# Attention and SwiGLU in one kernel: denominators of the first two batches by adds on VectorE, and a new order of gates and values in the front

## The chip, the cores and the metric

The kernel runs on one core of a Trainium2 chip. A core has a matrix engine (TensorE, PE in the profile; PEld is its loading of the stationary operand), three engines that work along rows (VectorE = DVE, ScalarE = ACT, GpSimd = POOL), a queue engine that issues transfers (SyncE = SP) and 16 DMA engines. Each engine takes its instructions in the order in which the program gives them. PE writes its results into eight PSUM banks; DVE and ACT take them out from there ("eviction"). The metric is the device time of one execution in microseconds; the time before the change is 232.76 us, the median of three runs (232.63 to 233.4).

## The reference

Eight batches, 8 heads, 576 positions, 64 features per head, 32 memory slots. Per batch and head:

```python
a   = exp(phi); a = a / sum over positions(a)         # phi: 576 x 32
k_m = a^T k;  v_m = a^T v                             # 32 x 64 each
s   = q k_m^T / 8;  attn = exp(s) / sum over the 32 slots
y   = attn v_m                                        # 576 x 64
```

(The reference also subtracts maxima, which cancel.) The heads' outputs of a position, side by side, are a row x of 512 numbers, 4608 rows in all, and then

```python
out = (silu(x w_gate) * (x w_val)) w_out              # w_gate, w_val: 512 x 1536, w_out: 1536 x 512
```

## The kernel before, in words

**Tiling.** The product of attention and gate or value weights is taken in another order: per batch, U = v_m W (256 rows of head and slot, by 1536 columns, for gate and value each; `u_round`, lines 460 to 502), and then gate^T = U^T attn^T. The 1536 columns come in three chunks of 512; chunk 0 of the weights is loaded in halves of 256 columns (four pieces: gate and value of the first half, then of the second), so that the first U can start earlier. Two row groups g of U (even and odd heads) sit in two banks and are evicted by two instructions; a string such as "va" says which engine takes which ("v" DVE, "a" ACT, with the scale 1/denominator of v_m in the same instruction for batches 0 and 1). `u_half` makes one half of chunk 0, `u_item` a whole chunk for gate and value.

A *slot* s of a batch (24 of them) is 128 of the 1536 columns by 288 positions. `gv_gate` (line 524) multiplies its gate (two matmuls, one for each g) and lets ACT take the silu into a tile `t_sg`, of which there are eight; it then puts a closure into a list `pend`, which, when called, multiplies the value (two matmuls) and lets DVE form silu x value into `t_h`. `flush_mul(n)` calls the oldest n of the list. `gv_slot` makes a gate and then calls what was pending before it, so that gates and values alternate on PE, one slot apart.

**Order of the work.** The program is a hand-written sequence (`manual_schedule`): the order of the Python calls is the order on each engine. Banks are handed out from a list first in, first out (`bank`, `done`, lines 75 to 84), so a bank comes round again after eight uses; `warm` gives its bank back to the front of the list. `warm(n)` (line 862) issues matmuls of the constant block matrix `bones` whose result nobody reads, four of n 128-wide units in each.

**Loads.** phi of batches 0 and 1 goes over the SP and ACT queues. All else is issued by POOL, in this order: k0, q0, k1, q1, v0, v1, the four pieces of chunk 0 (gate, value, gate, value), chunks 1 and 2 of the weights, w_out in three parts with k, phi and v of batch 2 in between. From the ninth of these loads on, POOL waits ahead of an issue until the load eight places earlier has landed.

**Front (batches 0 and 1).** `phi_exp_masked` (line 181) lets ACT write the exponentials of phi into a tile with a zero half: for each j of 9 and each g of 2, 128 columns (4 head pairs x 32 slots), of which only the 64 rows of head g are filled. `kv_denominators` (line 239) sums them for these two batches by 18 matmuls with a vector of ones, and `k_items` takes reciprocals; `direct` multiplies k or v with the exponentials by 36 matmuls into transposed form, which DVE copies to `t_kT`. `q_T` transposes q on PE (three groups of six) and copies it out. `scores` makes q k_m^T and ACT the exponentials E. The inverse sums over the 32 slots come in two ways: `z_inv` (line 418) sums by a matmul with `bones` and lets ACT take ln, ln and exp(-x); `z_inv_v` (line 431) does it on DVE by a summing transpose, a reciprocal and a transpose. `norm` (line 450) multiplies E by the inverse sum into `t_A`. Then come U and the slots of both batches, g0 for batch 0 and g1 for batch 1 (lines 946 to 965), and the third stage: the output product by sums and differences of blocks of `t_h` and `w_out` (`sums`, `weight_sums`, `products`, a seven-product scheme), beside which batches 2 to 7 run.

`phi_sum` (line 205) is there already for later batches: it adds the nine blocks of exponentials on POOL in FP32 and splits the sum into a bf16 high part and a bf16 rest (`t_ehl`), so that the denominators need two matmuls.

The lines around the change are 885 to 966 of the kernel. What decides the order there is this list:

```python
    run([u_half(0, (0,), 0, 0, "va")])
    norm(1, 1)
    run([u_half(0, (1,), 0, 0, "va"), u_half(1, (0, 1), 0, 0, "av")])
    for s in range(4):
        gv_gate(0, s)
    flush_mul(2)
    for s in range(2):
        gv_gate(1, s)
        flush_mul(1)
    run([u_half(0, (0, 1), 0, 1, "va"), u_half(1, (0, 1), 0, 1, "aa")])
    flush_mul(2)
```

Of the kernel before, what the change touches and what calls it, by code (L numbers as in the profile page):

```python
# [9 lines left out]
FP32 = mybir.dt.float32  # L10
BF16 = mybir.dt.bfloat16
# [3 lines left out]
def kernel(  # L15
# [147 lines left out]
    bones = consts.tile([128, 128], BF16, tag="bones", name="bones")  # L163
    ones1 = consts.tile([128, 1], BF16, tag="ones1", name="ones1")
    ones2 = consts.tile([128, NG], BF16, tag="ones2", name="ones2")
# [39 lines left out]
    def phi_sum(b):  # L205
# [14 lines left out]
        esums[b] = hl  # L220

    def kv_sum(b, p, parts):

# [15 lines left out]
    def kv_denominators(b, p):  # L239

        if b in masked:
            for g in range(NG):
                for j in range(JK):
                    nc.tensor.matmul(
                        p[:, g:g + 1],
                        lhsT=masked[b][:, j, g].rearrange("p i m -> p (i m)"),
                        rhs=ones1,
                        start=(j == 0),
                        stop=(j == JK - 1),
                    )  # L250
            return
        if b in esums:
            hl = esums.pop(b)
            terms = [hl[:, t] for t in range(2)]
        else:
            terms = [ephis[b][:, j].rearrange("p i m -> p (i m)") for j in range(JK)]
        for n, x in enumerate(terms):
            nc.tensor.matmul(p, lhsT=x, rhs=ones2, start=(n == 0), stop=(n == len(terms) - 1))
# [190 lines left out]

    def norm(b, g):  # L450
        a = att.tile([128, 2, HALF], BF16, tag=f"A{g}", name="t_A")
        nc.vector.tensor_tensor(out=a, in0=es.pop((b, g)), in1=lzs.pop((b, g)), op=ALU.mult)  # L452
        atts[b, g] = a
# [407 lines left out]

    def warm(n, narrow=0):

# [5 lines left out]
        for a in sizes:  # L869
            nc.tensor.matmul(  # L870
                p[:, 0:128 * a],
                lhsT=bones,
                rhs=x.to_broadcast([128, a, 128]) if a > 1 else bones,
                start=True,
                stop=True,
            )
# [9 lines left out]
    nc.vector.memset(bones, 0.0)  # L886
    nc.vector.memset(ones1, 1.0)
    nc.vector.memset(ones2, 0.0)
# [14 lines left out]
    for c in range(1, NCH):  # L903
        for which in range(2):
            load_w(which, c)
    load_wo(0)
    load_k(2)
    load_wo(1)
    load_phi(2, nc.gpsimd)
    load_wo(2)  # L910
    load_v(2)
    for c in range(NCH):
        u_buffer(1, c, f"S{c}")


    warm(104)
    k0, k1 = k_items(0, "vvvv"), k_items(1, "vvvv")
    q0, q1 = q_items(0, "vav"), q_items(1, "vav")
    run(k0)
    warm(8)  # L920
    run(k1[:1])
    run(q0)
    warm(4)
    scores(0, 0)
# [4 lines left out]
    z_inv(0, 1)  # L929
    norm(0, 0)  # L930
    warm(12)
    run(q1)
    norm(0, 1)
    warm(8)
# [4 lines left out]
    warm(8)  # L939
    z_inv(1, 1)  # L940
    norm(1, 0)
    warm(16)
# [5 lines left out]
    nc.scalar.preload_act_table_set("silu_and_others")  # L948
    run([u_half(0, (0,), 0, 0, "va")])
    norm(1, 1)  # L950
    run([u_half(0, (1,), 0, 0, "va"), u_half(1, (0, 1), 0, 0, "av")])
    for s in range(4):
        gv_gate(0, s)
    flush_mul(2)
    for s in range(2):
        gv_gate(1, s)
        flush_mul(1)
    run([u_half(0, (0, 1), 0, 1, "va"), u_half(1, (0, 1), 0, 1, "aa")])
    flush_mul(2)
    run(g1[2:4] + g0[4:8] + g1[4:6])  # L960
    for c in range(1, NCH):
        s = 8 * c
        run([u_item(0, c)] + g1[s - (2 if c == 1 else 3):s] + g0[s:s + 5])
        run([u_item(1, c)] + g0[s + 5:s + 8] + g1[s:s + 5])
    run(g1[-3:])
# [147 lines left out]
```

## Time and profile before

| what | us |
|---|---|
| median of three runs | 232.76 (232.63 to 233.4) |
| the profiled execution | 232.59, of which the span is 230.8 |
| PE busy | 222.3 (96%) |
| DVE busy | 184.8 (80%) |
| ACT busy | 171.6 (74%) |
| POOL busy | 145.1 (63%) |
| first product with w_out on PE | 54.07 |

The span runs from the first to the last instruction; 1.8 us of the measured time lie outside it. PEclk is the clock that TensorE was granted, in tenths. A row of the timeline gives start, length, engine, line, operation, what is written from what is read, shape and count; in brackets stands how long the engine had been idle before it and what ended that. The rows of groups give busy time in us and the mean of one instruction in ns. Instructions of one row may overlap, so that the length of a row with xN is that of the whole run of N.

### The profile page before, as it was taken

Reading aid. Unit: us, or ns where it says so; the run is one execution under the profiler, and the core shown is the slowest. Engines: PE = TensorE matmul, PEld = TensorE weight load, DVE = VectorE, ACT = ScalarE, POOL = GpSimd, SP = SyncE. Lnnn points to the kernel's source line nnn. Section 1 sums busy time; section 2 is a strip of 40 time slices with the busy share of each in tenths; the row PEclk is TensorE's granted clock in tenths of the full one; section 3 lists DMA queues with packets and bytes.
Section 4 is the critical chain, followed back from the end, with each engine's and each line's share of the span. In section 5 each row is a group of like instructions: output and inputs, shape, how many; then the busy total and the mean of one; then the engine's idle time right before and its main releaser. Section 6 shows DMA issues by size and latency. Waiting matters only on the chain.

```text
span 230.8 us, 7191 instructions
## 1 busy us (share of the span) xinstructions
PE 222.3 (96%) x2818; PEld 169.7 (74%) x2818; DVE 184.8 (80%) x423; ACT 171.6 (74%) x365; POOL 145.1 (63%) x197
## 2 busy tenths in 40 slices
PE   6997799999999999999999999999999999999993
PEld 2554476778887777878788787887788778878882
DVE  4056789999976799989997668998999899977832
ACT  2858898988547989968896658978898789677310
POOL 8422427998099759765977689464845394029291
PEclk9999999999999999999999999999999999999999
DMA  6999999999996993999299964996022602202024
GB/s 213 209 211 206 199 207 207 216 250 266 207 210 176 258 257 69 224 204 177 78 214 195 230 137 110 253 231 101 18 76 102 116 0 95 87 7 91 23 93 162
DMA packets 36546, 36.84 MB, mean 160 GB/s; under 512 B 14496, under 2 KB 30880, under 8 KB 36512
## 3 DMA queue, kind: packets, MB, share of 16 engines
q0 software_dynamic: 16272, 22.42, 52.7%
q1 hardware_dynamic: 19712, 13.37, 22.8%
q10 hardware_dynamic: 528, 0.59, 0.8%
q8 instruction: 22, 0.36, 0.6%
q14 instruction: 12, 0.10, 0.1%
HBM read 42.47 MB, written 9.44 MB: 225 GB/s over the span
## 4 chain that ended last, share of the span: by engine, by line
PE 87%; DMA 9%; POOL 2%; issue 0%; DVE 0%; POOLq 0%
PE p_os L723 21%; PE p_g L515 21%; PE p_v L515 20%; PE p_oc L723 10%; DMA W<-in_moe_w_val_dram 9%; PE p_oa L723 5%; PE p_u L472 5%; PE p_kv L230 2%; PE p_g L396 1%; POOL t_kv L99 1%; POOL t_kv L103 1%; PE p_q L383 1%; POOL t_q L108 0%; POOL W L138 0%; DVE t_q L339 0%
## 5 line engine op out<-in xcount | busy, mean ns | idle before, releaser
L538 DVE TENSOR_TENSOR t_h<-t_sg,p_v 128x288 bf16<-128x288 bf16 x192 | 81.7, 451 | 14.3 <-PE p_v L515 7.3
L515 PEld LDWEIGHTS <-t_U 128*128 128x128 bf16 x768 | 73.9, 98 | 21.2 <-issue 3.5
L532 ACT ACTIVATE t_sg<-p_g 128x288 bf16<-128x288 f32 x192 | 73.2, 424 | 17.2 <-PE p_g L515 11.4
L515 PE MATMUL p_g<-t_A,t_U 128*128 128x288 bf16 x384 | 77.0, 286 | 0.0
L515 PE MATMUL p_v<-t_A,t_U 128*128 128x288 bf16 x384 | 76.9, 286 | 0.0
L723 PEld LDWEIGHTS <-t_S 128*128 128x128 bf16 x384 | 37.3, 98 | 4.5 <-issue 0.2
L603 POOL TENSOR_TENSOR t_S<-t_h 128x512 bf16<-128x512 bf16 x17 | 19.6, 1154 | 27.7 <-DVE t_h L538 26.4
L723 PEld LDWEIGHTS <-t_h 128*128 128x128 bf16 x288 | 27.1, 98 | 8.6 <-issue 5.0
L492 ACT CAST t_U<-p_u 128x512 bf16<-128x512 f32 x51 | 27.0, 606 | 6.4 <-PE p_u L472 6.4
L723 PE MATMUL p_os<-t_T,t_S 128*128 128x256 bf16 x192 | 23.7, 273 | 0.0
L560 POOL TENSOR_TENSOR t_S<-t_S,t_h 128x512 bf16<-128x512 bf16 x17 | 19.6, 1155 | 1.3
L560 POOL TENSOR_TENSOR t_S<-t_h 128x512 bf16<-128x512 bf16 x16 | 18.4, 1152 | 0.0
L560 POOL TENSOR_TENSOR t_S<-t_h,t_S 128x512 bf16<-128x512 bf16 x16 | 18.4, 1151 | 0.0
L472 PE MATMUL p_u<-W,t_kT 64*32 64x512 bf16 (+1 forms) x416 | 15.3, 363 | 1.2 <-DMA W<-in_moe_w_val_dram 0.6
L870 PE MATMUL p_warm<-bones 128*128 128x512 bf16 x44 | 13.6, 450 | 1.7 <-DVE bones L892 1.7
L496 DVE CAST t_U<-p_u 128x512 bf16<-128x512 f32 x21 | 13.6, 683 | 1.9 <-PE p_u L472 1.9
L723 PE MATMUL p_os<-t_T,t_h 128*128 128x256 bf16 x96 | 14.8, 273 | 0.0
L452 DVE TENSOR_TENSOR t_A<-t_E,t_lz 128x576 bf16<-128x576 bf16 x16 | 11.4, 739 | 0.7 <-ACT t_lz L428 0.7
L723 PE MATMUL p_oc<-t_T,t_S 128*128 128x256 bf16 x96 | 11.9, 273 | 0.0
L723 PE MATMUL p_oa<-WO,t_h 128*128 128x256 bf16 x96 | 11.8, 273 | 0.0
L723 PE MATMUL p_oc<-WO,t_S 128*128 128x256 bf16 x96 | 11.8, 273 | 0.0
L723 PE MATMUL p_os<-WO,t_h 128*128 128x256 bf16 x96 | 11.8, 273 | 0.0
(108 smaller groups left out, 312.5 us busy)
## 6 DMA issues: line engine op xcount, KB each, us to landing
out_dram<-t_o SPq DMA_DIRECT2D x11, 512.0 KB, 3.3
t_kv<-in_k_dram POOLq DMA_DIRECT2D x8, 576.0 KB, 10.7
t_q<-in_q_dram POOLq DMA_DIRECT2D x8, 576.0 KB, 8.7
t_kv<-in_v_dram POOLq DMA_DIRECT2D x8, 576.0 KB, 15.1
t_phi<-in_phi_dram POOLq DMA_DIRECT2D x6, 576.0 KB, 8.5
out_dram<-t_o SPq DMA_DIRECT2D x10, 256.0 KB, 3.8
WO<-in_moe_w_out_dram POOLq DMA_DIRECT2D x3, 512.0 KB, 19.4
W<-in_moe_w_gate_dram POOLq DMA_DIRECT2D x2, 512.0 KB, 16.5
```

What stands on the lines that cost most here:

```text
L230: nc.tensor.matmul(p[g][32 * i:32 * i + 32, 0:n], lhsT=phi_of(b, g, j, i), rhs=kvs[b][64 * g:64 * g + 64, w0:w1, i, j * D:(j + 1) * D], st ...
L452: nc.vector.tensor_tensor(out=a, in0=es.pop((b, g)), in1=lzs.pop((b, g)), op=ALU.mult)
L472: nc.tensor.matmul(p[g][32 * i:32 * i + 32, o:o + n], lhsT=kTs[b][64 * g:64 * g + 64, 2, 32 * i:32 * i + 32], rhs=w_part(w, c, i, g, halve ...
L492: nc.scalar.copy(out=t, in_=p)
L496: nc.vector.tensor_copy(out=t, in_=p)
L515: nc.tensor.matmul(p[:, 0:HALF], lhsT=Us[b, c, g][:, o // 2, which, 128 * (o % 2):128 * (o % 2 + 1)], rhs=atts[b, g][:, r], start=(g == 0) ...
L532: nc.scalar.activation(out=sg, in_=gate[:, 0:HALF], func=AF.Silu)
L538: nc.vector.tensor_tensor(out=dst, in0=sg, in1=val[:, 0:HALF], op=ALU.mult)
L560: eng.tensor_tensor(out=out, in0=x, in1=y, op=ALU.subtract)
L603: eng.tensor_tensor(out=t[:, 0], in0=A21, in1=A22, op=ALU.add)
L723: nc.tensor.matmul(mine[home][:, u], lhsT=lhs(c, m, u), rhs=rhs(c, m), start=fresh and u == 0, stop=(k == 5), skip_group_check=u == 1 or n ...
L870: nc.tensor.matmul(p[:, 0:128 * a], lhsT=bones, rhs=x.to_broadcast([128, a, 128]) if a > 1 else bones, start=True, stop=True,)
```

## The change

- The denominators of batches 0 and 1: a new function `phi_sum_masked` adds the two halves of the masked tile (one of them zero for each row) and then the nine blocks on DVE, by five adds, a copy and a subtraction, and `kv_denominators` multiplies the two parts with `ones2`, as for later batches. The 18 matmuls per batch and `ones1` go. The product of k comes ahead of the denominators in both batches.
- The first warm-up is 16 instead of 26 matmuls and has `ident` as its stationary operand.
- q of batch 1: all three copies on DVE (before, the middle one on ACT).
- The second inverse sum of batch 1 goes from `z_inv` to `z_inv_v`. `norm(0, 0)` moves behind the copies of q of batch 1, `norm(1, 1)` to POOL, `norm(1, 0)` behind the first U.
- The loads of w_out and of k, phi and v of batch 2 move behind `norm(1, 1)` on POOL.
- Chunk 0: the gate halves of U of both batches come first (evicted "aa" and "vv"), then four gates of batch 0, the value halves ("vv" and "aa"), four gates of batch 1, four values, the second halves, four values.
- Chunk 1: U for the gates of both batches, four gates of batch 0, U for the values, three gates of batch 1, and then seven values in a row.

```diff
@@ -161,7 +161,6 @@
 
     ident = consts.tile([128, 128], BF16, tag="ident", name="ident")
     bones = consts.tile([128, 128], BF16, tag="bones", name="bones")
-    ones1 = consts.tile([128, 1], BF16, tag="ones1", name="ones1")
     ones2 = consts.tile([128, NG], BF16, tag="ones2", name="ones2")
 
 
@@ -217,6 +216,28 @@
         hl = att.tile([128, 2, 128], BF16, tag="ehl", bufs=1, name="t_ehl")
         nc.gpsimd.tensor_copy(out=hl[:, 0], in_=t[:, 0])
         nc.gpsimd.tensor_tensor(out=hl[:, 1], in0=t[:, 0], in1=hl[:, 0], op=ALU.subtract)
+        esums[b] = hl
+
+    def phi_sum_masked(b):
+
+        u = att.tile([128, JK, NP, M], BF16, tag="ephi", name="t_ephi")
+        e = u.rearrange("p j i m -> p j (i m)")
+        z = masked[b].rearrange("p j g i m -> p j g (i m)")
+        t = att.tile([128, 4, 128], FP32, tag="es", bufs=1, name="t_es")
+        hl = att.tile([128, 2, 128], BF16, tag="ehl", bufs=1, name="t_ehl")
+        for out, x, y, op in (
+            (e, z[:, :, 0], z[:, :, 1], ALU.add),
+            (t, e[:, 0:4], e[:, 4:8], ALU.add),
+            (t[:, 0:2], t[:, 0:2], t[:, 2:4], ALU.add),
+            (t[:, 0], t[:, 0], t[:, 1], ALU.add),
+            (t[:, 0], t[:, 0], e[:, 8], ALU.add),
+            (hl[:, 0], t[:, 0], None, None),
+            (hl[:, 1], t[:, 0], hl[:, 0], ALU.subtract),
+        ):
+            if y is None:
+                nc.vector.tensor_copy(out=out, in_=x)
+            else:
+                nc.vector.tensor_tensor(out=out, in0=x, in1=y, op=op)
         esums[b] = hl
 
     def kv_sum(b, p, parts):
@@ -238,17 +259,6 @@
 
     def kv_denominators(b, p):
 
-        if b in masked:
-            for g in range(NG):
-                for j in range(JK):
-                    nc.tensor.matmul(
-                        p[:, g:g + 1],
-                        lhsT=masked[b][:, j, g].rearrange("p i m -> p (i m)"),
-                        rhs=ones1,
-                        start=(j == 0),
-                        stop=(j == JK - 1),
-                    )
-            return
         if b in esums:
             hl = esums.pop(b)
             terms = [hl[:, t] for t in range(2)]
@@ -447,9 +457,9 @@
         )
         lzs[b, g] = lz
 
-    def norm(b, g):
+    def norm(b, g, eng=nc.vector):
         a = att.tile([128, 2, HALF], BF16, tag=f"A{g}", name="t_A")
-        nc.vector.tensor_tensor(out=a, in0=es.pop((b, g)), in1=lzs.pop((b, g)), op=ALU.mult)
+        eng.tensor_tensor(out=a, in0=es.pop((b, g)), in1=lzs.pop((b, g)), op=ALU.mult)
         atts[b, g] = a
 
 
@@ -859,7 +869,7 @@
     def gv_slots(b):
         return [lambda s=s: gv_slot(b, s) for s in range(2 * NJF)]
 
-    def warm(n, narrow=0):
+    def warm(n, narrow=0, lhs=None):
 
 
         p = bank([128, DM], FP32, "p_warm")
@@ -869,7 +879,7 @@
         for a in sizes:
             nc.tensor.matmul(
                 p[:, 0:128 * a],
-                lhsT=bones,
+                lhsT=bones if lhs is None else lhs,
                 rhs=x.to_broadcast([128, a, 128]) if a > 1 else bones,
                 start=True,
                 stop=True,
@@ -884,7 +894,6 @@
     load_q(0)
     load_k(1)
     nc.vector.memset(bones, 0.0)
-    nc.vector.memset(ones1, 1.0)
     nc.vector.memset(ones2, 0.0)
     for g in range(NG):
         nc.vector.memset(ones2[64 * g:64 * g + 64, g:g + 1], 1.0)
@@ -903,23 +912,20 @@
     for c in range(1, NCH):
         for which in range(2):
             load_w(which, c)
-    load_wo(0)
-    load_k(2)
-    load_wo(1)
-    load_phi(2, nc.gpsimd)
-    load_wo(2)
-    load_v(2)
     for c in range(NCH):
         u_buffer(1, c, f"S{c}")
 
 
-    warm(104)
+    phi_sum_masked(0)
+    warm(64, lhs=ident)
     k0, k1 = k_items(0, "vvvv"), k_items(1, "vvvv")
-    q0, q1 = q_items(0, "vav"), q_items(1, "vav")
-    run(k0)
+    q0, q1 = q_items(0, "vav"), q_items(1, "vvv")
+    run(k0[1:])
     warm(8)
-    run(k1[:1])
+    run(k0[:1])
+    warm(8)
     run(q0)
+    phi_sum_masked(1)
     warm(4)
     scores(0, 0)
     scores(0, 1)
@@ -927,9 +933,10 @@
     z_inv(0, 0)
     run(k1[1:])
     z_inv(0, 1)
-    norm(0, 0)
+    run(k1[:1])
     warm(12)
     run(q1)
+    norm(0, 0)
     norm(0, 1)
     warm(8)
     scores(1, 0)
@@ -937,8 +944,7 @@
     v_direct(0, "vvvv")
     z_inv(1, 0)
     warm(8)
-    z_inv(1, 1)
-    norm(1, 0)
+    z_inv_v(1, 1)
     warm(16)
     v_direct(1, "vvvv")
     warm(8)
@@ -946,22 +952,38 @@
 
     g0, g1 = gv_slots(0), gv_slots(1)
     nc.scalar.preload_act_table_set("silu_and_others")
-    run([u_half(0, (0,), 0, 0, "va")])
-    norm(1, 1)
-    run([u_half(0, (1,), 0, 0, "va"), u_half(1, (0, 1), 0, 0, "av")])
+    run([u_half(0, (0,), 0, 0, "aa")])
+    norm(1, 1, nc.gpsimd)
+    load_wo(0)
+    load_k(2)
+    load_wo(1)
+    load_phi(2, nc.gpsimd)
+    load_wo(2)
+    load_v(2)
+    norm(1, 0)
+    run([u_half(1, (0,), 0, 0, "vv")])
     for s in range(4):
         gv_gate(0, s)
-    flush_mul(2)
-    for s in range(2):
+    run([u_half(0, (1,), 0, 0, "vv"), u_half(1, (1,), 0, 0, "aa")])
+    for s in range(4):
         gv_gate(1, s)
-        flush_mul(1)
+    flush_mul(4)
     run([u_half(0, (0, 1), 0, 1, "va"), u_half(1, (0, 1), 0, 1, "aa")])
-    flush_mul(2)
-    run(g1[2:4] + g0[4:8] + g1[4:6])
-    for c in range(1, NCH):
-        s = 8 * c
-        run([u_item(0, c)] + g1[s - (2 if c == 1 else 3):s] + g0[s:s + 5])
-        run([u_item(1, c)] + g0[s + 5:s + 8] + g1[s:s + 5])
+    flush_mul(4)
+    run(g0[4:8] + g1[4:6])
+    for b in range(2):
+        u_round(b, (((0,), 1, (0, 1)),), "av")
+    run(g1[6:8])
+    for s in range(8, 12):
+        gv_gate(0, s)
+    for b in range(2):
+        u_round(b, (((1,), 1, (0, 1)),), "va")
+    for s in range(8, 11):
+        gv_gate(1, s)
+    flush_mul(7)
+    run(g0[12:16] + g1[11:13])
+    run([u_item(0, 2)] + g1[13:16] + g0[16:21])
+    run([u_item(1, 2)] + g0[21:24] + g1[16:21])
     run(g1[-3:])
     flush_mul()
     backlog = []
```

## The prediction

> **What bounds the kernel now.** I read the page first (busy shares, clock, DMA), then the chain that ended last, then the timeline from 24 to 33 us, where the chain goes over from a transfer to TensorE. The page:
>
> ```profile
> span 230.8 us, 7191 instructions
> PE 222.3 (96%) x2818; PEld 169.7 (74%) x2818; DVE 184.8 (80%) x423; ACT 171.6 (74%) x365; POOL 145.1 (63%) x197
> PEclk9999999999999999999999999999999999999999
> GB/s 213 209 211 206 199 207 207 216 250 266 207 210 176 258 257 69 224 204 177 78 214 195 230 137 110 253 231 101 18 76 102 116 0 95 87 7 91 23 93 162
> ```
>
> The first five slices (5.8 us each) move a flat 199 to 213 GB/s: up to about 27 us the loads set the pace. The chain says the same: the second weight piece is on its way until 26.66 us, and from there everything is TensorE.
>
> ```profile
> 6.03 0.72 POOL W L138
> 6.74 19.88 DMA W<-in_moe_w_val_dram
> 26.66 0.52 PE p_u L472 x24
> 27.19 1.09 PE p_g L515 x8
> 28.27 0.49 PE p_v L515 x4
> ...
> 29.74 0.56 PE p_u L472 x32
> ```
>
> The table by stretches shows that nothing is idle on PE afterwards, and that DVE and ACT are nearly full beside it:
>
> ```profile
> 34.00:36.00 2.00, 2.00 (x29) 1.13 (x28) 1.93 (x5) 1.72 (x4) 0.74 (x1) 1.00 1.24 205
> 40.00:42.00 2.00, 2.00 (x19) 1.59 (x17) 2.00 (x6) 1.96 (x6) 2.00 (x4) 1.00 1.25 213
> ```
>
> (columns: stretch, its length, busy PE, PEld, DVE, ACT, POOL with counts, clock, DMA, GB/s). So the change can move the end only by what it does to the moment from which PE is full, or by a hole that it tears into the full stretch. The handover, in order of time:
>
> ```profile
> 24.64 0.98 DVE L339 CAST t_kT<-p_mT 64x64 bf16<-64x64 f32 x4 [0.49 <-PE p_mT L325]
> 24.69 1.28 ACT L948 ACT_TABLE_LOAD   x1
> 25.73 0.30 PE L472 MATMUL p_u<-W,t_kT 64*32 64x256 bf16 x8 [0.58 <-DVE t_kT L339]
> 25.88 0.74 POOL L153 DMA_DIRECT2D WO<-in_moe_w_out_dram  x1 [1.17 <-DMA W<-in_moe_w_gate_dram]
> 26.12 0.47 ACT L494 ACTIVATE t_U<-p_u,t_rS 128x256 bf16<-128x256 f32 x1 [0.15 <-PE p_u L472]
> 26.66 0.52 PE L472 MATMUL p_u<-W,t_kT 64*32 64x256 bf16 x24 [0.63 <-DMA W<-in_moe_w_val_dram]
> 27.06 1.05 ACT L494 ACTIVATE t_U<-p_u,t_rS 128x256 bf16<-128x256 f32 x2 [0.46 <-PE p_u L472]
> 27.12 1.16 PE L515 MATMUL p_g<-t_A,t_U 128*128 128x288 bf16 x8
> 28.00 1.94 ACT L532 ACTIVATE t_sg<-p_g 128x288 bf16<-128x288 f32 x6
> 28.63 1.67 DVE L538 TENSOR_TENSOR t_h<-t_sg,p_v 128x288 bf16<-128x288 bf16 x4 [0.34 <-PE p_v L515]
> ```
>
> POOL's next issue waits for the first gate piece and starts at 25.88. Where PE and POOL wait for one load, POOL starts 0.24 later (v of batch 0: 20.91 and 21.15; of batch 1: 23.73 and 23.97), so that piece lands at 25.64 for PE, 0.09 before PE uses it. By 27.19 all 32 first-half products of U are done and the gates run. A gate or value of one slot (two matmuls) takes 0.245 us, a block of 32 U products 0.56, entering such a block 0.09 (29.33+0.245 to 29.67). Counting on from 27.12: after 64 U products and 16 gates or values PE stands at **31.72** (10 by 29.67, U to 30.24, 6 more). From there 80 gates and values and 64 wide U products follow without a hole.
>
> **The change, part by part.**
>
> Start: the warm-up needs ident (POOL, done at 4.02) in place of bones (1.73), and has 16 matmuls instead of 26. In the trace the first 12 come 0.43 apart, later ones 0.21: 4.1 + 12 x 0.43 + 4 x 0.21 = 10.1, the same end as now (10.1). k of batch 0 is there at 9.30. Nothing. The Trainium skill (TensorE: Matmul & The Clock Gate, "What's actually happening") speaks against a later start: full clock comes only after a window of about 3.4 us of sustained activity that runs freely. By it the end would lie near 9 to 10, also covered.
>
> Denominators: 36 matmuls (two runs of 0.59) leave PE, 4 of two columns (0.04 each by p_kv L258, 0.37 for 9) come. PE waits for loads there: nothing gained. DVE gets 2 x 7 instructions that the trace has only on POOL. Nearest DVE rows:
>
> ```profile
> L753 DVE TENSOR_TENSOR t_o<-p_os,t_p 128x512 f32<-128x512 f32 x8 | 5.5, 687 | 3.6 <-ACT t_p L748 2.9 <-PE p_os L723 0.5
> L790 DVE TENSOR_TENSOR t_p<-p_os,t_p 128x256 f32<-128x256 f32 x2 | 0.8, 421 | 1.3 <-PE p_os L723 1.3
> L560 DVE TENSOR_TENSOR t_T<-WO 128x512 bf16<-128x512 bf16 x6 | 2.5, 416 | 0.0
> ```
>
> 512 and 256 elements in f32 give 1.04 ns per element on top of 0.15; bf16 at 0.416 goes twice as fast. So 1152 bf16: 0.75 (1.35 if it does not get the fast form); 512 to f32: 0.69; 256: 0.42; four of 128: 0.29 each. Sum 3.0, upper end 3.6; I take 3.0.
> DVE's queue with it: exponentials of batch 0 ready 8.2, sum to 11.2, k copies (1.21) 12.45, reciprocal and scale 12.85, two q copies 13.95, second sum 17.0, k copies 18.2, reciprocal and scale 18.6, three q copies (one of them from ACT) 20.15, two norms 21.65, v copies 22.7, inverse sum of (1,1) on DVE (0.77+0.27+0.78) 24.55. The v copies of batch 1 still start at 24.64, since v lands at 23.7. Nothing, with 0.1 us to spare; behind that, a later DVE costs only from about 1 us on, because its next item on the path (the value halves of U) is due at 28.4. Scores of batch 1 come near 20.2 (now 19.72); ACT loses ln, ln, exp (1.45) and has its table by about 25, before U needs it.
>
> Norm of (1,1) on POOL: POOL rows grow by 2.1 ns per element (L212: 128 f32 0.454, 256 0.725), so 576 is 1.40; from 24.7 to 26.1, needed at 28.3. Queued behind it are the loads of WO, k2, phi2, v2: WO moves from 25.88 to 26.1, with six weight transfers still in flight and its first use at 54. Nothing. A DVE add beside POOL's copies at 55.3 took 0.66 instead of 0.42, so norm (1,0) may stretch by some 0.25. The Trainium skill (SBUF — State Buffer, "Who interferes with whom") goes further: with two SBUF inputs DVE waits out the whole POOL instruction. That would be 0.5 here, inside the 1 us of cover.
>
> Gates ahead of values, first chunk, which is the path. U gate half of batch 0 still waits for 25.64; both its evictions go to ACT, one after the other: 26.12 + 0.43 + 0.47 = 27.02 (0.43 is 1.05 less 0.62 for a 512-wide one). The second matmul of the first gate needs the second: **27.1**. Now the same gate ran at 27.12, with all 32 U products behind it; then 16 are. So: 7 matmuls to 27.96, U values 0.09+0.28 to 28.33, four gates of batch 1 to 29.31; values need U evicted by DVE twice (28.41+0.92=29.33): 29.35 to 30.33; second half of U, batch 0: 30.42 to 30.70. Batch 1 takes the banks of the last two gates, free when ACT has done its queue: four silus from 27.47, two U evictions, four silus, the last ending at 30.92 at the spacing of 0.31 (28.00 row), at 31.3 with 0.37 (8 in 2.98 at 31.91). So U from 30.95 to 31.24, four values to **32.2**: 0.5 after 31.72. Without the bank wait it is +0.25, with slow silus +0.9.
>
> Second chunk: gates of both batches (7) come ahead of their values; both U blocks stay at two entries. Eight gates wait for their product at a time, which is what the sg tiles allow; bunched evictions may hold the seven values up: lower end 0, upper 0.4 (one U eviction by ACT, 0.6, less the 0.2 by which PE comes later); I take 0.1, since at 0.31 per silu every bank is just free. DVE has 25.1 us of work after its first product (28.63 to 54.92 less 1.2 idle); started at 29.75 it ends near 55 to 55.4, within the shift of PE.
>
> Sum: +0.5 +0.1 = **+0.6 us**. The profiled execution took 232.59 (span 230.8 and 1.8 around it), 0.17 under the median 232.76; I put the shift on the median: 233.36, say 233.4. Later stages are full of PE and carry it to the end.
>
> **Rivals.**
> Same: banks and evictions come in time, +0.25 or less, down to -0.25 if U starts at 25.64 and its second eviction is quicker. For it: the slacks are tenths. Against: 16 U products lie behind 27.1.
> Much slower: the DVE queue does not hold. It decides once each sum takes over 3.5 us: the value halves of U then come late, and with 3.6 to 4 us, or adds slowed by POOL as at 55.3, it costs 0.4 to 1.0 more, together with a full ACT in chunk two 233.8 to 234.8.
> Faster: the first gate piece lands earlier than 25.64. It must do so by 1.3 us to reach -0.7; the time would be near 232.0. For it: fewer instructions and later loads beside it. Against: its issue (6.01) and what is queued ahead of it are unchanged, at a flat 200 GB/s.
>
> **How the numbers follow.** 0.3% (0.7 us) is about what a measurement of this kernel can tell from no change. Forecast, +0.25 to +1.0: 0.55, of it 0.25 above +0.7. Same: 0.15. Much slower: 0.20. Faster: 0.10. So slower 0.25+0.20, same 0.30+0.15, faster 0.10. Range: 232.6 (the lower bounds) to 234.5.
>
> **What would show it.** Right: the first gates near 27.1, U values behind four gates, first product on DVE near 29.8 instead of 28.63, a gap on PE in the second half of U near 30.8, and PE at its last value of batch 1 near 54.8 instead of 54.2. The DVE sums show at 8.2 and 14, 3 us each. Wrong: a U product before 25, or gates before 26.9 (faster); v copies of batch 1 after 26.5 or value evictions after 28.8 (much slower); DVE late in the stage from 54 to 63, where its sums of S and T feed PE.

## The result and the profile after

| | before | after |
|---|---|---|
| median, us | 232.79 (232.63 to 233.4) | 234.19 (233.78 to 234.86) |
| ratio, 95% interval | | 1.0069 (1.0056 to 1.0082) |
| profiled execution, us | 232.59, span 230.8 | 233.78, span 232.0 |
| first product with w_out on PE, us | 54.07 | 54.03 |
| PE busy between 54 and 66 us | 12.00 of 12 | 10.81 of 12 |

By the medians the change costs 1.40 us; the ratio would make it 1.6. Ratios go by the fast executions alone, and the only slow one among all the runs below is the 239.24 of e1. The forecast was 233.4, with a range of 232.6 to 234.5: the time lies in the range, above its middle, but the loss is not where the sum had put it, so that the hit is luck. The front, in which the forecast saw nearly all of it (0.5 of 0.6), is as fast as before. The page of the kernel after:

```profile
span 232.0 us, 7120 instructions
...
PE 220.4 (95%) x2776; PEld 167.7 (72%) x2776; DVE 193.0 (83%) x440; ACT 169.7 (73%) x362; POOL 146.9 (63%) x198
...
GB/s 212 211 210 207 198 207 206 222 243 270 202 192 174 225 271 89 202 194 224 23 216 227 192 174 87 253 245 108 0 93 94 120 4 90 80 13 93 23 88 162
```

The row of the clock is full (9 in every slice) and the first five slices are as flat as before (198 to 212 GB/s). The chain of the kernel after, cut to 24 to 31 us (start, length, what):

```profile
25.02 0.23 DVE t_kT L349
...
25.29 0.37 PE p_u L482 x8
25.66 0.84 ACT t_U L504 x2
...
26.55 1.03 PE p_g L525 x7
...
30.12 0.56 PE p_u L482 x32
```

The second weight piece is no longer on the chain. PE starts U at 25.29, behind a copy of t_kT, and both evictions by ACT are in the path, as the prediction had them. The timeline of the same stretch of after (start, length, engine, line, what; in brackets the idle time ahead and what ended it):

```profile
24.77 0.98 DVE L349 CAST t_kT<-p_mT 64x64 bf16<-64x64 f32 x4
24.89 1.28 POOL L462 TENSOR_TENSOR t_A<-t_E,t_lz 128x576 bf16<-128x576 bf16 x1
...
25.78 1.00 DVE L462 TENSOR_TENSOR t_A<-t_E,t_lz 128x576 bf16<-128x576 bf16 x1
...
29.49 1.55 DVE L548 TENSOR_TENSOR t_h<-t_sg,p_v 128x288 bf16<-128x288 bf16 x4 [0.73 <-PE p_v L525]
...
31.76 0.66 PE L525 MATMUL p_g<-t_A,t_U 128*128 128x288 bf16 x4
```

POOL's norm takes 1.28, w_out's first load goes out at 26.12, the first product on DVE is at 29.49. At 31.76 PE has done 64 U products and 16 gates and values. Before, that point was 31.72.

The table by stretches of after (stretch, its length, busy PE, PEld, DVE, ACT, POOL with counts, clock, DMA share, GB/s) shows where the time goes:

```profile
40.00:42.00 2.00, 2.00 (x18) 1.59 (x17) 2.00 (x7) 1.35 (x4) 1.92 (x3) 1.00 1.23 207
54.00:66.00 12.00, 10.81 (x193) 9.22 (x192) 10.49 (x26) 7.30 (x12) 6.49 (x11) 1.00 1.20 217
```

The same stretch of before, in the third stage, is full:

```profile
54.00:66.00 12.00, 12.00 (x204) 10.31 (x203) 10.01 (x27) 8.29 (x14) 5.37 (x9) 1.00 1.15 215
```

In after PE is full up to the third stage (22.00 of the 22 us from 32 to 54), and there 1.19 us are missing. The waits of PE in after name one wait there:

```profile
PE p_q L393 <- DVE t_bkv L276: 1.2, 1, 1.2
```

It does not occur before. The spans differ by as much: 232.0 less 230.8.

Why is `t_bkv` late? DVE's timeline of after ahead of it, cut to four rows (the scaling that writes `t_bkv` follows the reciprocal at 61.29):

```profile
54.79 0.95 DVE L613 TENSOR_TENSOR t_S<-t_h 128x512 bf16<-128x512 bf16 x1
55.77 0.53 DVE L570 TENSOR_TENSOR t_S<-t_S,t_h 128x512 bf16<-128x512 bf16 x1
...
57.39 0.86 DVE L570 TENSOR_TENSOR t_T<-WO 128x512 bf16<-128x512 bf16 x1
...
61.09 0.17 DVE L272 RECIPROCAL t_rS<-p_kv 128x2 f32<-128x2 f32 x1
```

and the same rows of before:

```profile
54.84 0.42 DVE L603 TENSOR_TENSOR t_S<-t_h 128x512 bf16<-128x512 bf16 x1
55.29 0.66 DVE L560 TENSOR_TENSOR t_S<-t_S,t_h 128x512 bf16<-128x512 bf16 x1
...
57.00 0.41 DVE L560 TENSOR_TENSOR t_T<-WO 128x512 bf16<-128x512 bf16 x1
...
59.92 0.16 DVE L262 RECIPROCAL t_rS<-p_kv 128x2 f32<-128x2 f32 x1
```

DVE begins these twelve adds at the same time (54.79 and 54.84) and is through with them 1.17 later. They are the same adds. In after seven of the twelve take 0.53 to 0.95 us; in before three take 0.64 to 0.66 and the other nine 0.41 to 0.43. What runs beside the longer ones is POOL. POOL's timeline of after:

```profile
38.98 1.15 POOL L613 TENSOR_TENSOR t_S<-t_h 128x512 bf16<-128x512 bf16 x1 [3.70 <-PE p_v L525]
...
54.30 1.15 POOL L570 TENSOR_TENSOR t_S<-t_h,t_S 128x512 bf16<-128x512 bf16 x1
...
57.52 1.62 POOL L602 COPY t_x<-t_h 128x256 bf16<-128x256 bf16 x3
```

and of before:

```profile
36.91 1.15 POOL L603 TENSOR_TENSOR t_S<-t_h 128x512 bf16<-128x512 bf16 x1 [1.28 <-PE p_v L515]
...
52.21 1.16 POOL L560 TENSOR_TENSOR t_S<-t_h,t_S 128x512 bf16<-128x512 bf16 x1
...
55.22 1.62 POOL L592 COPY t_x<-t_h 128x256 bf16<-128x256 bf16 x3
```

All of POOL's work is 2.1 to 2.3 us later: its last add of the block ended at 53.37, ahead of DVE's adds; now it ends at 55.45, beside them, and the copies run until 59.14 instead of 56.84. The delay starts with the very first sum, which waits 3.70 us for a value product on PE. PE's timeline of after shows which:

```profile
36.10 1.14 PE L525 MATMUL p_g<-t_A,t_U 128*128 128x288 bf16 x8
37.18 0.62 PE L482 MATMUL p_u<-W,t_kT 64*32 64x512 bf16 x16
37.73 0.91 PE L525 MATMUL p_g<-t_A,t_U 128*128 128x288 bf16 x6
38.48 1.27 PE L525 MATMUL p_v<-t_A,t_U 128*128 128x288 bf16 x9
```

`gv_slot` issues a gate and then the values that were pending before it, so the value of slot 7 of batch 1 stays pending. In the new order of chunk 1 the seven gates and a block of U come next, and that value is issued first of the run at 38.48. In before it came behind a single gate, at 36.41, which is 2.07 earlier:

```profile
36.16 0.41 PE L515 MATMUL p_g<-t_A,t_U 128*128 128x288 bf16 x2
36.41 0.41 PE L515 MATMUL p_v<-t_A,t_U 128*128 128x288 bf16 x2
```

This value is the last reader of U of batch 1, chunk 0. That tile was allocated with the tag `S0` (`u_buffer(1, c, f"S{c}")`), and `t_S` of batch 0, chunk 0, POOL's first sum, takes the next turn of the same tag (line 607). So the sum starts 0.5 us into that run of values.

### The profile page after: what moved, and what is told of

The parts are those of the page before. It is cut to its first block, busy times and chain, and to the rows that moved or that the text cites. A ratio compares the mean times of both kernels' runs of the same rounds, so it can differ in the third digit from the quotient of the medians.

```text
span 232.0 us, 7120 instructions
## 1 busy us (share of the span) xinstructions
PE 220.4 (95%) x2776; PEld 167.7 (72%) x2776; DVE 193.0 (83%) x440; ACT 169.7 (73%) x362; POOL 146.9 (63%) x198
## 4 chain that ended last, share of the span: by engine, by line
PE 82%; DMA 7%; DVE 6%; POOL 1%; issue 1%; ACT 1%; POOLq 0%
PE p_g L525 20%; PE p_os L733 20%; PE p_v L525 19%; PE p_oc L733 10%; DMA t_kv<-in_v_dram 7%; PE p_u L482 5%; PE p_oa L733 5%; DVE t_T L570 2%; PE p_kv L251 2%; DVE t_h L548 2%; PE p_g L406 1%; DVE t_S L570 1%; POOL t_kv L99 1%; DVE t_kT L349 1%; POOL t_q L108 0%
## 5 line engine op out<-in xcount | busy, mean ns | idle before, releaser
L525 PE MATMUL p_g<-t_A,t_U 128*128 128x288 bf16 x384 | 75.9, 286 | 0.1
L525 PE MATMUL p_v<-t_A,t_U 128*128 128x288 bf16 x384 | 75.3, 286 | 0.0
L733 PEld LDWEIGHTS <-t_h 128*128 128x128 bf16 x288 | 27.1, 98 | 8.6 <-issue 5.0
L482 PE MATMUL p_u<-W,t_kT 64*32 64x512 bf16 (+1 forms) x416 | 15.9, 364 | 0.1
L602 POOL COPY t_x<-t_h 128x256 bf16<-128x256 bf16 x24 | 11.8, 500 | 0.0
L462 DVE TENSOR_TENSOR t_A<-t_E,t_lz 128x576 bf16<-128x576 bf16 x15 | 10.8, 755 | 0.0
```

What stands on the lines that cost most here:

```text
L462: eng.tensor_tensor(out=a, in0=es.pop((b, g)), in1=lzs.pop((b, g)), op=ALU.mult)
L482: nc.tensor.matmul(p[g][32 * i:32 * i + 32, o:o + n], lhsT=kTs[b][64 * g:64 * g + 64, 2, 32 * i:32 * i + 32], rhs=w_part(w, c, i, g, halve ...
L525: nc.tensor.matmul(p[:, 0:HALF], lhsT=Us[b, c, g][:, o // 2, which, 128 * (o % 2):128 * (o % 2 + 1)], rhs=atts[b, g][:, r], start=(g == 0) ...
L602: nc.gpsimd.tensor_copy(out=xs[b // 2][:, 4 * c:4 * c + 4, :, b % 2].rearrange("p o (t r) -> p o t r", r=2), in_=hts[b, c].rearrange("p o ...
L733: nc.tensor.matmul(mine[home][:, u], lhsT=lhs(c, m, u), rhs=rhs(c, m), start=fresh and u == 0, stop=(k == 5), skip_group_check=u == 1 or n ...
```

## The experiments

Two theories stood at the start. **Late sums:** the shared buffer delays POOL by 2 us, POOL then runs beside DVE's adds at 55 to 59, and PE waits. **Front:** the new order of the front and of chunk 0 costs time that shows later. A third one came up with the first results. **Instruction blocks:** the change takes 84 PE instructions out (42 matmuls with their weight loads), and PE's program is fetched in blocks. All kernels were timed against the kernel before on the same chip; its median there was 232.66 (e1 to e4), 232.73 (e5 to e8, on another chip than the rest) and 232.71 (e9 to e12). Each trace is of one execution.

**e1: chunk 1 in its old order, all else as after.**

```diff
-    for b in range(2):
-        u_round(b, (((0,), 1, (0, 1)),), "av")
...
-    run(g0[12:16] + g1[11:13])
+    run([u_item(0, 1)] + g1[6:8] + g0[8:13])
+    run([u_item(1, 1)] + g0[13:16] + g1[8:13])
```

> The changed kernel with the second chunk in the old order (U for gate and value together, values one slot behind their gates); the first chunk and the rest of the change stay. Theory 'late sums': in the changed kernel the last value of batch 1 in chunk 0 comes 2 us later, it is the last reader of the buffer into which POOL writes its first sums (38.98 instead of 36.91), POOL's copies and issues then run beside DVE's sums at 55 to 59 and slow them, and PE waits 1.2 us for t_bkv at 60.7. By it the first sums are back near 36.9, no wait of PE on t_bkv, and 232.7 +- 0.3 us. Rival 'DVE front' (gates first and the sums on DVE leave DVE behind by the third stage): it stays at 234.0 or more. Rival 'bunched chunk' (seven gates and seven values in a row cost by themselves, through full banks and ACT): 232.7 too.

Measured: 234.11, ratio 1.0040 (1.0017 to 1.0063), eleven executions from 232.51 to 234.89, five of them below 232.7, and one at 239.24. The hole between 54 and 66 us is gone (PE busy 12.00) and POOL's sums start at 37.00. But most executions are no faster than after: a second loss appears. The profiled one (234.8) has it at 110 to 113 us. PE's weight loads stand still for 1.04 us with no releaser in the profile, PE for 0.73, and the next U then waits 1.1 for a transposed k. (The profile puts PE's 0.73 down to a silu of ACT, but ACT's run of six ended at 110.89, 0.29 ahead.) The weight loads, PE beside them, and U:

```profile
111.17 0.11 PEld L525 LDWEIGHTS <-t_U 128*128 128x128 bf16 x2 [1.04 <-issue]
111.18 0.42 PE L525 MATMUL p_v<-t_A,t_U 128*128 128x288 bf16 x2 [0.73 <-ACT t_sg L542]
...
113.40 0.84 PE L482 MATMUL p_u<-W,t_kT 64*32 64x512 bf16 x24 [1.10 <-DMA t_kT<-t_bkv]
```

**e2: the kernel before with the new order of chunk 1 alone.**

```diff
-    for c in range(1, NCH):
-        s = 8 * c
...
+    for b in range(2):
+        u_round(b, (((0,), 1, (0, 1)),), "av")
...
+    run(g0[12:16] + g1[11:13])
+    run([u_item(0, 2)] + g1[13:16] + g0[16:21])
+    run([u_item(1, 2)] + g0[21:24] + g1[16:21])
```

> The kernel before with nothing but the new order of the second chunk. 'Late sums': POOL's first sums start near 39, PE waits about 1.2 us for t_bkv near 60.7, 234.0 us (+1.2). 'DVE front': 232.8. 'Bunched chunk': 233.5 to 234, but with the loss between 35 and 54 us, so that the first product with w_out comes after 54.5.

Measured: 233.89 (233.73 to 234.01), ratio 1.0051 (1.0038 to 1.0064). POOL's sums start at 39.22. The stretch of e2 has the hole of after without any change in the front:

```profile
54.00:66.00 12.00, 10.83 (x193) 9.20 (x191) 10.71 (x26) 7.32 (x11) 6.57 (x10) 1.00 1.15 215
```

**e3: after, with `t_S` of batch 0, chunk 0 in a tile of its own** (one buffer fewer of `t_lz` makes room).

```diff
-        t = upool.tile([128, 4, 2, 256], BF16, tag=f"U{c}" if b == 1 else f"S{c}", name="t_S")
+        t = upool.tile([128, 4, 2, 256], BF16, tag=f"U{c}" if b == 1 else "S00" if (b, c) == (0, 0) else f"S{c}", name="t_S")
```

> The changed kernel with all its orders, but POOL's first sums are written to a tile of their own instead of the buffer that U of batch 1, chunk 0 has held (room for it comes from two instead of three tiles lz). 'Late sums': POOL starts its first sums near 35.5, as soon as the products of batch 0 are there, its work is done before 55, PE does not wait for t_bkv, 232.6 +- 0.3. 'DVE front' and 'bunched chunk': nothing changes, 234.0 to 234.3.

Measured: 233.82, ratio 1.0048 (1.0021 to 1.0076), from 232.38 to 235.09. The new order of chunk 1 is all there, and the hole is gone (12.00): POOL starts its sums at once behind its load of v (34.64 to 35.38).

```profile
35.40 1.16 POOL L613 TENSOR_TENSOR t_S<-t_h 128x512 bf16<-128x512 bf16 x1
```

So the buffer is what delays POOL, not the order as such. Its spread is that of e1, with the same losses near 111 us in the profiled execution.

**e4: the kernel before, POOL delayed by two more adds of 1.2 us behind its first sums.**

```diff
             sums(nc.gpsimd)
+            if (b, c) == (0, 0):
+                for n in range(2):
+                    fill = att.tile([128, 2, 256], BF16, tag="fill", bufs=1, name="t_fill")
+                    nc.gpsimd.tensor_tensor(out=fill, in0=A11, in1=A12, op=ALU.add)
```

> The kernel before with two more adds of 128x512 on POOL (2.2 us, into a tile that nobody reads) behind its first sums; nothing else. 'Late sums': POOL's later work moves by 2.2 us into the stretch of DVE's sums, those take about 1.2 us longer in all, PE waits for t_bkv, 233.9 to 234.1. 'DVE front' and 'bunched chunk': POOL is not on the path, 232.8.

Measured: 234.01 (233.97 to 234.31), ratio 1.0061 (1.0049 to 1.0073). Nothing of the change is in this kernel; a POOL that is 2.3 us late (its copies end at 59.36) makes the whole loss. PE waits 1.2 us for `t_bkv`, as in after. The stretch of e4:

```profile
54.00:66.00 12.00, 10.78 (x191) 9.04 (x190) 10.71 (x26) 7.10 (x11) 6.58 (x10) 1.00 1.15 215
```

e2, e3 and e4 settle the hole. Left over was why e1 and e3 are not at 232.7. The trace lists transfers of 16 KB on a queue of the kind instruction: 22 in the kernel before, 21 after. Before, PE runs 5636 matmuls and weight loads, which makes 256 for each, so these are taken for the fetches of PE's program, in blocks of 256. Set beside the transposing transfer of q in the fourth stage (us; from the transfers' records):

```
kernel                       q transposed on SP     fetch before   fetch behind its start
before                       100.22 to 106.88           88.37       101.22, 107.67
e1                           100.36 to 108.66           91.68       108.63
e3                           100.17 to 108.60           91.50       108.45
after                        101.41 to 107.37           93.25       107.28
```

In before one fetch starts 1.0 us after the transfer was issued, ahead of its first packet (103.07). In the three kernels with 84 instructions fewer no fetch starts until the transfer is at its end (0.03 to 0.15 us ahead of it). The reading: the fetch was due meanwhile and had to wait; in e1 and e3 PE ran out of instructions at about 110. The count of PE's matmuls and weight loads fits the first half of it: 486 lie between these two fetches in e1 and in e3, 441 in after, and 261 between 88.37 and 101.22 in before. But a late fetch alone costs nothing. In before 454 lie between the fetches at 68.84 and 83.44, where no transposing transfer runs, and PE does not wait. The next four runs test the reading.

**e5: e1, with 84 PE instructions put back.** The first warm-up keeps its columns, but 56 of its 64 units of 128 columns are matmuls of their own.

```diff
-    warm(64, lhs=ident)
+    warm(64, narrow=56, lhs=ident)
```

> The changed kernel with the second chunk in the old order, and the first warm-up in 58 matmuls instead of 16, with the same number of columns: 42 matmuls and 42 weight loads more, as many as the change took out of PE's program. Theory 'instruction blocks': PE's program comes in blocks of 16 KB (256 instructions); with 84 instructions less, the refill that should come near 102 us falls into the DMA transpose of q for batch 5 and waits for its end (108.9), and PE runs dry at 110.4 in part of the executions (232.5 to 239.2 with the same order and 16 matmuls). By it the executions lie close together again, within 0.5 us, at 232.6 +- 0.2. Rival 'transfers': what makes the slow executions is the timing of loads and stores that the front has shifted, and the spread of 2 us and more stays.

Measured: 233.1 (232.77 to 233.74, and one at 235.48), ratio 1.0024 (1.0006 to 1.0042). That is 1.0 less than e1 at the median, and the fetch comes at 101.6 again. But the expectation was missed, in the median and in the spread, the intervals of the two ratios overlap, and e1's five lowest times lie under all of e5's: this run alone decides nothing.

**e6: the kernel before, with 172 PE instructions more**, so that its blocks are cut where those of after are cut.

```diff
-    warm(104)
+    warm(104, narrow=104)
...
-    warm(8)
+    warm(8, narrow=8)
...
-    warm(4)
+    warm(4, narrow=2)
```

> The kernel before with 172 more instructions on PE, all in the first warm-ups (the same columns in narrower matmuls), so that its blocks are cut as in the changed kernel (256 - 84 = 172). 'Instruction blocks': up to 60 us nothing changes, and part of the executions become slow, 233.5 to 235, with a spread of 1 us or more. 'Transfers': 232.7 as before, close together.

Measured: 233.2 (232.69 to 233.73, and one at 235.25), ratio 1.0024 (1.0007 to 1.0042): slower than before with nothing of the change, and wider, with three of the twelve executions above 233.5. Again no fetch starts inside the transfer of q (100.47 to 107.36) until its end, at 107.3. PE does not run dry near 110 in the profiled execution.

**e7: after, with the same 84 instructions put back** (the edit of e5).

> The changed kernel with the 84 instructions put back into the first warm-up, nothing else. Late sums of POOL stay, the instruction blocks are cut as before: by both theories together 233.8 +- 0.2, close together, against 233.78 to 234.86 of the changed kernel. If the blocks have nothing to do with it, the spread of 1 us stays.

Measured: 234.17 (233.84 to 234.42), ratio 1.0058 (1.0046 to 1.0070), hole as in after (10.82). The median lies above what was expected and nothing is gained: as long as the hole is there, the blocks do not show in the time of after. The spread is 0.6 us instead of 1.1, from five and six executions.

**e8: e5, with the gate halves of U evicted by ACT and DVE side by side** and `norm(1, 0)` behind them.

```diff
-    run([u_half(0, (0,), 0, 0, "aa")])
+    run([u_half(0, (0,), 0, 0, "av")])
...
+    run([u_half(1, (0,), 0, 0, "av")])
     norm(1, 0)
-    run([u_half(1, (0,), 0, 0, "vv")])
```

> As e5, and the first U evicted by ACT and DVE side by side for both batches, the norm of (1,0) behind them on DVE. In the changed kernel the first gates wait from 25.9 to 26.55 for the second eviction on ACT; side by side they can go on at 26.2. 'The front has no slack left' (PE is full from the first gates on): 0.3 to 0.4 us less than e5, 232.2 to 232.3, first product with w_out near 53.7 instead of 54.05. Rival 'evictions bound it' (ACT and DVE set the pace of the first chunk): as e5.

Measured: 232.63 (232.5 to 233.48), ratio 0.9998 (0.9989 to 1.0006): the kernel before again, no faster, and 0.3 more than was expected. The first product with w_out is at 53.92, 0.28 earlier than in e5.

**e9: after, with the tile of e3 and the instructions of e5.** All of the change is in it.

> The changed kernel, with t_S of batch 0, chunk 0 in a tile of its own (no buffer shared with U of batch 1, one lz buffer fewer), and 84 PE instructions put back as narrower warm-up products of the same total width. Late sums alone: POOL's first sums start at 35 to 37 us, PE has no wait on t_bkv in 54 to 66 us (busy 12.0 us there), and with the instructions put back nothing else is lost: 232.5 to 233.0. Instruction blocks alone (the buffer doesn't matter): as the changed kernel with 84 instructions put back, 234.0 to 234.4. If both the hole is gone and the median stays at 233.5 or above, a third cause is at work that neither names.

Measured: 232.69 (232.48 to 233.46), ratio 1.0000 (0.9992 to 1.0009). Against e7 this is one tile's difference, and it is 1.48 us (on two chips; by the ratios to before 1.35). POOL's first sum is at 35.59, and the stretch of e9 is full:

```profile
54.00:66.00 12.00, 12.00 (x205) 10.46 (x204) 9.81 (x28) 8.59 (x15) 3.62 (x6) 1.00 1.17 216
```

So the change without the shared buffer and with its instruction count kept is worth nothing, to 0.1%.

**e10: the kernel before, with 256 PE instructions more**, one whole block, so that all later blocks are cut as before.

```diff
-    warm(104)
+    warm(104, narrow=104)
...
-    warm(8)
+    warm(8, narrow=8)
...
-    warm(12)
+    warm(12, narrow=12)
...
-    warm(16)
+    warm(16, narrow=14)
```

(all five `warm(8)`.)

> The kernel before with 256 more PE instructions, one whole block of its instruction transfers (16 KB), from the same warm-up columns cut into narrower products: from the warm-ups on every block is cut where it was cut in the kernel before. Instruction blocks: it is the place of the cut that counts, so 232.6 to 232.9, executions close together, against 233.2 and a range of 3 us for the 172 added instructions. Rival, the number of instructions or the narrower warm-ups cost time by themselves: 233.2 or more, with executions as far apart as there.

Measured: 233.1 (232.94 to 233.21), ratio 1.0017 (1.0008 to 1.0026). The executions do lie close together, 0.3 us against 2.6 in e6, with a fetch at 101.5 inside the transfer of q (100.57 to 106.65). The median misses what was expected by 0.2. In the profiled execution that is the front: the first product with w_out is at 54.37 (before 54.07), behind a wait of 1.1 for the second weight piece (before 0.6), and the lag of 0.35 at 114.96 against 114.61 stays that to the end. Either the more numerous narrow warm-ups are not free, or this is the scatter of that load, which with the old warm-ups let U go on at 26.64 to 26.84 (e4, before, e2) and here at 26.96. It bears on e6 too: part of its 0.5 may be this, since its first product was at 54.33.

**e11: e5 with 48 instructions more**, which puts the fetch ahead of the transfer of q.

```diff
-    warm(64, narrow=56, lhs=ident)
+    warm(64, narrow=64, lhs=ident)
...
-    warm(8)
+    warm(8, narrow=8)
```

(three of the `warm(8)`.)

> The changed kernel with the old order of chunk 1 and 84 + 48 PE instructions more than the changed kernel has: the block that was fetched at 101.8 us with 84 is due about 3 us earlier, at 98 to 99 us, before the transposing transfer of q begins at 100.4. Instruction blocks: 232.5 to 232.9, executions close together. Rival, transfers of this order collide whatever the blocks: median near 233.1 and executions 2 to 3 us apart, as with 84.

Measured: 233.9 (233.75 to 234.97), ratio 1.0061 (1.0046 to 1.0076). The fetch did come at 98.45, before the transfer began at 100.51, and the time was a microsecond over what was expected. The expectation fell. The trace shows PE waiting once more with no releaser, one stage on: the next transposing transfer of q runs from 124.36 to 131.85, a fetch starts at 131.81, and PE's weight loads stand still, PE itself for 0.48 of the 0.8 us by which the profiled span is longer than that of e5 (232.0 and 231.2). PE's row among the waits, and the weight load:

```profile
PE p_os L733 <- issue: 0.5, 1, 0.5
...
134.20 0.10 PEld L733 LDWEIGHTS <-t_Q 128*128 128x128 bf16 x1 [0.67 <-issue]
```

**e12: e8 with the same 48 instructions more.**

> The same 48 instructions more, with the halves of U's first chunks evicted by ACT and DVE side by side and the norm of batch 1 behind them (232.63 without the 48). Instruction blocks: 232.3 to 232.6, executions close together, 0 to 0.3 us less than the kernel before, as the first w_out product at 53.9 us is 0.15 earlier. Rival: 232.6 or more and as spread as without the 48, since that version's blocks were not late.

Measured: 233.62 (232.84 to 234.21), ratio 1.0040 (1.0025 to 1.0054), 1.0 more than e8; the expectation fell here too. The larger part is another wait, for a transposed k, as in e1:

```profile
112.23 0.84 PE L482 MATMUL p_u<-W,t_kT 64*32 64x512 bf16 x24 [0.95 <-DMA t_kT<-t_bkv]
```

The transposing transfer of q ahead of it on the same queue took 7.18 us (e8: 6.26), so that of k went out at 107.53 (e8: 106.44). PE stands without a releaser for 0.21 at 134.46.

What the second group settles: the number of PE instructions changes the time by 0.8 to 1.1 us with the work unchanged (e5 against e11, e8 against e12, e3 against e9). In e1, e3, e11 and e12 PE is seen waiting with no releaser, and each of the four waits ends 2.4 to 2.6 us after a fetch began; this speaks for missing instructions. It is a part of the loss only: in e1, e3 and e12 PE waits longer for the transposed k (1.1, 1.2 and 0.95 us against 0.73, 0.8 and 0.21), which goes out behind the transfer of q. The transfers of q in the fourth stage took 6.0 to 8.4 us in these runs; what sets that, and whether the instruction count does, stays open. Nor is there a rule for where the blocks must fall: putting one fetch ahead of one transfer moved the loss to the next.

## Why the prediction was right or wrong, point by point

| step | predicted | shown in after |
|---|---|---|
| end of the first warm-up | 10.1 | 9.73 |
| sums of exponentials on DVE, each | 3.0 | 3.1 |
| their first add of 1152 bf16 | 0.75 | 0.76 |
| v copies of batch 1 start | 24.64 | 24.77 |
| norm of (1,1) on POOL | 1.40 | 1.28 |
| norm (1,0) on DVE beside it | 0.75 + 0.25 | 1.00 |
| first gates | 27.1 | 26.55 |
| 64 U products and 16 gates and values | 32.2 | 31.76 |
| loss from chunk 0 | +0.5 | 0.0 |
| loss from chunk 1 and later | +0.1 | +1.2 |

**What bounds the kernel:** right. PE is full from 32 us on in both kernels, apart from a hole that the change tears; the prediction said that only the start of the full stretch or such a hole can move the end.

**The moved work in the front:** right. The warm-up ends 0.4 early, the rest is priced to 0.15 us: DVE's queue held with two sums in it, POOL's norm and the later loads cost nothing. On the norm beside POOL's the row was right: 1.00 measured. The full wait of the Trainium skill (SBUF — State Buffer, "Who interferes with whom") would have given 1.25 by the forecast's times, and 1.14 by those of after (POOL's norm ends at 26.17, DVE's began at 25.78).

**Chunk 0, +0.5: wrong.** The failed step is "that piece lands at 25.64 for PE". It was inferred from the start of POOL's next issue. In after U starts at 25.29, as soon as two copies of t_kT are done, and the piece was there. From then on the counting was good: two evictions by ACT (0.84; the sum had 0.90), gates 0.06 behind them, everything 0.5 earlier. The wait for a bank in the second half did not come either: the four values take 1.15 to the next gate, where 0.98 is the plain price. Over the kernels run, the first U of the new front starts between 25.29 and 25.92 (in e9 it waits 0.8 for the piece), so the term was smaller than the scatter of that load. The profiled execution of e9, with the piece this late, has the loss that the sum forecast: its first product with w_out is at 54.53, 0.46 behind before. The median of e9 does not.

**Chunk 1, +0.1: wrong, and this is what made the loss.** The failed step is the one that ends in "I take 0.1". It looked at ACT, the banks and DVE's queue, gave the late values to DVE, and did not ask who else waits for a value that is held back. Behind the value of slot 7 of batch 1 stands a buffer, and behind the buffer POOL's first sum, which started 2.07 us later. POOL's part was closed with "Nothing" after its loads. The price followed from rows of before: POOL's block of work runs from 36.91 to 56.84 with a single wait at its head, so any delay there arrives in full at 53 to 57, where DVE's adds start. The trace already had adds of 0.66 and 0.64 instead of 0.42 there, beside POOL's copies, and the prediction used one of them for the norm at 26 us, but not where it stood.

**The rivals.** "Much slower" named 233.8 to 234.8 and holds the result, but its condition, sums over 3.5 us, did not occur: they took 3.1. Of its two mechanisms the second, "adds slowed by POOL as at 55.3", is the one that acted, in the third stage and on other adds. "Faster" asked for a first piece 1.3 us earlier; it was 0.35 or more, which made up for the front's loss and no more. The last of the signs of being wrong, "DVE late in the stage from 54 to 63, where its sums of S and T feed PE", named the right place, but had no price and no cause in the sum. Slower came out, by 1.40 instead of 0.6, from a term that the sum did not have, while the term that made up most of the 0.6 did not come. That the time still lies in the range is luck.

**What is left.** The hole is 1.19 of the 1.40 us between the medians; the two profiled executions differ by just 1.19. The remaining 0.2 (0.4 by the ratio) is within the spread of the executions (233.78 to 234.86) and was not traced to a cause.

## What to carry to other kernels

Where a change holds back an instruction, list the readers of every tile that it reads last: in a kernel with shared tags the one who waits is the next owner of the buffer, often on an engine that the change never touches. An engine with slack hands such a delay on in full as long as its work has no gap in it, so follow it to where its work meets that of the engine on the path. And when instructions are taken out or added, allow for the count itself: with the same work a different number of PE instructions was worth up to 1.1 us here, and putting the count back (e3 against e9) tells that effect from the change's own.

## What the runs showed of the hardware

- DVE adds of two tiles in SBUF (128x512, bf16, 0.42 us alone) took 0.53 to 0.95 us beside POOL's adds, copies and issues, the twelve of them 6.3 us instead of 5.1. The Trainium skill (SBUF — State Buffer, "Who interferes with whom") has the later of two such instructions wait out the whole of the earlier: the add at 54.79 would then take 0.66 (POOL's add ends at 55.45) and 0.42, together 1.08, the one at 55.77, beside a copy that ends at 56.07, 0.72. Measured were 0.95 and 0.53, so the rule has the direction and is too long by 0.1 to 0.2. The first add of e4, with POOL's add beside it until 55.68, agrees: 1.15 measured, 1.29 by the rule.
- PE can stand still in straight code with no releaser in the profile: its weight loads did for 1.04 us in e1, 1.09 in e3, 0.67 in e11 and 0.40 in e12. Each time this ended 2.4 to 2.6 us after a 16 KB fetch had begun, and in the first three the fetch began within 0.2 us of the end of a transposing transfer (in e12 0.8 behind it). The Trainium skill (Runtime: NRT & Kernel Launch, "Instruction fetch mechanics") calls the cost of crossing a 16 KB boundary mostly hidden. In the kernel before it is: PE has no such wait in its list.
- In the one profiled execution of e10, with the warm-up's columns split over 128 more matmuls, the second weight piece let U go on at 26.96 instead of 26.66. With the warm-ups unsplit it was 26.64 in e4 and 26.84 in e2, so up to 0.2 of the 0.3 is scatter, and whether the split moves the load is not shown.
